# Block 0's first root among the second half's work, and two weight conversions behind the low parts, by a table of issue places

## The chip, the cores and the metric

The kernel runs on one core of a Trainium2 chip. The metric is the time of one execution on the device, in microseconds (us); lower is better. A core has a matrix engine (PE, TensorE), a vector engine (DVE), a scalar engine (ACT), a general engine (POOL, GpSimd) and SP, whose queue issues all the transfers (DMAs) of this kernel. Each engine takes its instructions in the order in which the program issues them; between engines there are only semaphores.

## The reference

Three stages follow each other: attention over 2 x 8 heads of 768 positions (a local window and one key per block of 32), a gated layer with a root-mean-square norm, and a second layer with an ELU.

```python
def _moe_ref(x, w_gate, w_val, w_out, rms_g):
    rms = np.sqrt(np.mean(x * x, axis=-1, keepdims=True) + 1e-06)
    xn = x / rms * rms_g
    g = xn @ w_gate
    silu = g * (1.0 / (1.0 + np.exp(-g)))
    return (silu * (xn @ w_val)) @ w_out          # 1536 tokens, 512 -> 1536 -> 512

def _moe2_ref(x, w_in, w_out):
    h = x @ w_in                                  # 512 -> 2048 -> 512
    return np.where(h > 0.0, h, np.exp(np.minimum(h, 0.0)) - 1.0) @ w_out
```

## The kernel before

**Blocks.** The 1536 tokens are three blocks of 512 columns, with the model dimension on the partitions. Block 0 goes through attention first. Its two halves of 256 tokens (`slice(0, 256)` and `slice(256, 512)`, called the first and the second half here) enter the gated layer as soon as each is there. Blocks 1 and 2 go through attention under the matmuls of block 0, and later through the two layers together.

**The gated layer on block 0.** Every float32 operand is cut into a high and a low part: `x_hi` (ACT or DVE) and `x_lo` (DVE) for the tokens, `split_a` (ACT) and `split_b` (POOL or DVE) for the weights. `project` multiplies high by high, high by low and low by high, 12 matmuls of 128 x 256 for one half of 256 tokens. The first products of chunks 0 and 1 run a half at a time, in PSUM banks of their own: `pv0_1c`, `pv0_0c`, `pg0_1`, and later `pg0_0`.

**The root.** The norm's factor for one half is computed in a row of small steps, `add_norm`: `square` (ACT), `sum_square` (PE, 16 float32 matmuls with 4 columns, bank `m0`), `mean_square` (DVE, frees the bank), `root` (POOL, a power), `diagonal` (DVE, two instructions), `spread` (PE, two float32 matmuls, bank `t0` for the first half and `t1` for the second), `keep_root` (DVE, copies the factor to `rk0` and frees the bank). On block 0 the factor is first used by `gate_r`, which needs both halves.

**The weights.** They come as 64-bit floats. `fetch` (SP) loads a piece into one of five buffers `st`; `convert_a` (ACT), `convert_b` and `convert_d` (DVE) make a 32-bit word of it in a buffer `raw`. `convert_b` writes the word from the upper half of the 64 bits; `convert_d` adds the lowest bits from the lower half, and is the last to read the `st` buffer. `keep` (SP) writes the word to memory for the later blocks, and `split_a`, `split_b` make the parts for the matmuls.

**What sets the order.** `Order.issue` (lines 82 to 217) plays the steps through on a timetable of costs and due times before anything is emitted, notes the order in which they start (`started`), and then calls them in that order. The order of these calls is the order of each engine's instructions. The semaphores are put in by the tile framework, from the order of the calls too: a step waits for every earlier call that wrote what it reads, or that read or wrote what it writes; a buffer passes on when all the steps of its last tile are done. The bank of each tile is the one that the timetable chose.

**The order around the change.** On PE: `turn_e` of pair 3, `sum_square` (first half), `scores` of pair 4 (banks `t0`, `t1`), `apply_v2` of pair 3, `pv0_1c` (first half), `spread` (first half, bank `t0`), `pv0_0c` and `pg0_1` (first half), `pv0_0c` and `pg0_1` (second half), `turn_e` of pair 4 twice, `sum_square` (second half), `pg0_0` (first half), `apply_v2` of pair 4 (bank `t0`), `spread` (second half), `pg0_0` (second half). On DVE: `convert_b` of v0, g1, g0, then `convert_d v 0`, `convert_d g 0`, the four `x_lo` of the first half with `mean_square` between, `convert_d g 1`, `diagonal`, `add_mask`, `row_max`, `keep_root`, `row_max`, the four `x_lo` of the second half. On ACT, `split_a` of g1 stands before the four `x_hi` of the second half. `keep v 0`, `split_a` and `split_b` of v0 are called right behind `convert_d v 0`, ahead of the last `x_lo`.

Of the kernel before, what the change touches and what calls it, by code (L numbers as in the profile page):

```python
# [43 lines left out]
class Order:  # L44
# [18 lines left out]
    def add(self, engine, cost, due, fn, *args, r=(), w=(), new=()):  # L63

        due += SHIFT.get((fn.__name__, sum(due >= x for x in EDGES)), 0)
        self.ops.append((engine, cost, due, fn, args, tuple(r), tuple(w), tuple(new)))
# [15 lines left out]
    def issue(self):  # L82
        ops = self.ops
        n = len(ops)
        before = [set() for _ in range(n)]
        writer, readers, home, maker, users = {}, {}, {}, {}, {}
        queue = {}
        for i, (engine, _, due, _, _, r, w, new) in enumerate(ops):
            for tag, name in new:
                home[name] = tag  # L90
                if tag in self.slots and self.slots[tag][1]:
                    queue.setdefault(tag, []).append((due, i, name))
            for key in r:
                before[i].add(writer[key])
                readers.setdefault(key, []).append(i)
            for key in w:
                if key in writer:
                    before[i].add(writer[key])
                before[i].update(readers.pop(key, ()))
                writer[key] = i  # L100
            before[i].discard(i)
            for name in {key.split("#")[0] for key in (*r, *w)} | {name for _, name in new}:
                if name in home:
                    before[i].add(maker.setdefault(name, i))
                    users.setdefault(name, set()).add(i)
            before[i].discard(i)
        queue = {tag: [name for _, _, name in sorted(x)] for tag, x in queue.items()}
        after = [[] for _ in range(n)]
        left = [len(b) for b in before]
        for i, b in enumerate(before):  # L110
            for j in b:
                after[j].append(i)

        ready_at = [op[2] if op[0] in ("SP", "-") else 0.0 for op in ops]
        free = {tag: bufs for tag, (bufs, _) in self.slots.items()}
        busy, soon, started, port = dict(self.busy), {}, [], 0.0
        dma_free = now = 0.0
        events = [(t, -1, 0) for t in (*ready_at, *busy.values()) if t > 0]
        heapq.heapify(events)
        taken = [None] * n  # L120
        ticks = {}
        tiled = 0

        def offer(i):
            for engine in ops[i][0] if isinstance(ops[i][0], dict) else (ops[i][0],):
                soon.setdefault(engine, []).append(i)

        for i in range(n):
            if not left[i]:
                offer(i)  # L130


        def pick(i):
            need, found = {}, []
            for tags, name in ops[i][7]:
                for tag in tags if isinstance(tags, tuple) else (tags,):
                    n = need.get(tag, 0) + 1
                    if free[tag] >= n and (not self.slots[tag][1] or name in queue[tag][:n]):
                        break
                else:  # L140
                    return None
                need[tag] = n
                found.append((tag, name))
            return found

        def can(i):
            return pick(i) is not None

        def shared(i, engine):
            return engine in ("DVE", "POOL") and ops[i][3].__name__ in SHARED  # L150

        while len(started) < n or events:
            for engine in list(soon):
                if busy.get(engine, 0.0) > now + 1e-9:
                    continue
                todo = sorted((i for i in soon[engine] if taken[i] is None), key=lambda i: (ops[i][2], i))
                best = next((
                    i for i in todo if ready_at[i] <= now + 1e-9 and can(i)
                    and (not shared(i, engine) or port <= now + 1e-9)), None)
                if best is None:  # L160
                    continue
                where, cost, due, _, _, _, _, new = ops[best]
                if isinstance(where, dict):
                    cost = where[engine]
                look = now + self.look * cost
                if engine != "SP" and any(
                        ops[i][2] < due - self.urgent and now < ready_at[i] <= look and can(i) for i in todo):
                    continue
                taken[best] = engine
                for e in where if isinstance(where, dict) else (where,):  # L170
                    soon[e].remove(best)
                for tag, name in pick(best):
                    home[name] = self.tag_of[name] = tag
                    free[tag] -= 1
                    if self.slots[tag][1]:
                        queue[tag].remove(name)
                if engine == "SP":
                    dma_free = max(now + self.DMA_START, dma_free) + cost
                    busy[engine] = now + self.ISSUE.get(ops[best][3].__name__, 0.42)
                    end = dma_free + self.DONE.get(ops[best][3].__name__, self.DMA_DONE)  # L180
                else:
                    if engine == "PE":
                        name = ops[best][3].__name__
                        start = now
                        if TILED.get(name, 0) != tiled:
                            tiled = TILED.get(name, 0)
                            start += DRAIN_IN if tiled else DRAIN_OUT
                        end = self.pe_end(start, cost, LIGHT.get(name, 1.0), ticks)
                    else:
                        end = now + cost  # L190
                    busy[engine] = end
                if shared(best, engine):
                    port = end
                heapq.heappush(events, (end + (0.2 if engine == "PE" else 0.13), best, 1))
                heapq.heappush(events, (busy[engine], -1, 0))
                started.append(best)
                for j in after[best]:
                    left[j] -= 1
                    ready_at[j] = max(ready_at[j], end + self.hop(engine, ops[j][0]))
                    if not left[j]:  # L200
                        offer(j)
                        heapq.heappush(events, (ready_at[j], -1, 0))
            if not events:
                stuck = [(e, [(ops[i][2], ops[i][3].__name__, ops[i][4][:3]) for i in t[:3]]) for e, t in soon.items()]
                raise RuntimeError(f"no group can start: {stuck} {free}")
            now, i, ends = heapq.heappop(events)
            if ends:
                for name in {key.split("#")[0] for key in (*ops[i][5], *ops[i][6])} | {x for _, x in ops[i][7]}:
                    if name in users:
                        users[name].discard(i)  # L210
                        if not users[name]:
                            del users[name]
                            free[home[name]] += 1
        for i in started:
            ops[i][3](*((taken[i],) if isinstance(ops[i][0], dict) else ()), *ops[i][4])
        return now


# [1 line left out]
def fused_kernel(ctx: ExitStack, tc: tile.TileContext, q, k, v, w_gate, w_val, w_out, rms_g, w_in2, w_out2, out):  # L220
# [720 lines left out]
    def add_act(src, dst, due, tag="act"):  # L941
        h, l = dst + "h", dst + "l"
        add(ANY_SB, 0, due, act_a, src, dst, tag, r=[src], w=[h], new=[(tag, h)])
        add(ANY_2[ACT_B if "act1_0" in dst else 0], 0, due + 0.6, act_b, src, dst, tag, r=[src, h], w=[l], new=[(tag, l)])

# [641 lines left out]
X_0 = 23.0, 30.0  # L1587
WARM_AT = (3.4, 3.9, 4.0, 7.5, 8.5, 9.5, 10.5, 13.0)
AFTER_K, WARM_LONG = {1: 0, 2: 2}, {1: 8}
ACT_B = 0  # L1590
LO_0, LO_1 = (1, 1, 0), 0
LEN_A, LEN_2, LEN_U, LEN_P = 9.3, 6.3, 9.7, 1.37
# [40 lines left out]
```

## Time and profile before

| | us |
|---|---|
| median of 3 runs | 590.31 |
| lowest and highest | 589.7, 591.51 |
| the profiled execution | 590.2 |
| its span, first to last instruction | 588.4 |

The profile is one execution. Times in it are counted from the first instruction. What lies around the span is 1.8 us. A row of the timeline gives start, duration, engine, line, operation, result and operands, how many instructions are merged in it, and in brackets the idle time before it with what ended it. Buffer numbers are left out of the names, so that `pv_0c` is `pv0_0c`, `pg` is any `pg0_n`, and a tile of the root shows as the slice in its name.

### The profile page before, as it was taken

What the parts mean: (1) busy time and instruction counts of PE and PEld (TensorE: products, weight loads), DVE (VectorE), ACT (ScalarE), POOL (GpSimd) and SP (SyncE); (2) the same over time, 40 slices, a digit from 0 to 9 for tenths busy, and PEclk for the clock granted to TensorE, in tenths of its full rate; (3) what the DMA queues carried; (4) which work ended last, traced back from release to release, by engine and by line L of the source; (5) the groups of instructions that cost most, each with busy time, mean ns of one, the idle gap of its engine ahead of it and who ended that gap; (6) DMA issues with size and microseconds to landing.
All of it is one profiled execution on the core that took longest, in us unless ns stands there. A gap on an engine that the chain in (4) does not pass through costs nothing.

```text
span 588.4 us, 10067 instructions
## 1 busy us (share of the span) xinstructions
PE 575.3 (98%) x3382; PEld 469.9 (80%) x3382; DVE 543.4 (92%) x1048; ACT 408.4 (69%) x888; POOL 97.1 (17%) x144
## 2 busy tenths in 40 slices
PE   7899999999999999999999999999999999999997
PEld 3688877888888888888888888788888888888886
DVE  4999988889999997999989888999999999999994
ACT  4887749755989888375455446596667599977651
POOL 5655466453311104000000000000000000000000
PEclk9999999999999999999999999999999999999999
DMA  9688997769778699223533453331206625816021
GB/s 318 227 282 299 321 381 279 252 204 298 251 260 299 230 378 342 99 101 116 178 107 108 144 164 123 90 108 55 72 19 206 187 73 173 261 58 207 1 72 53
DMA packets 56052, 108.80 MB, mean 185 GB/s; under 512 B 6784, under 2 KB 19584, under 8 KB 56000
## 3 DMA queue, kind: packets, MB, share of 16 engines
q1 hardware_dynamic: 56000, 108.16, 55.4%
q8 instruction: 26, 0.43, 0.3%
q14 instruction: 26, 0.21, 0.1%
HBM read 79.82 MB, written 28.31 MB: 184 GB/s over the span
## 4 chain that ended last, share of the span: by engine, by line
PE 87%; DVE 7%; ACT 3%; issue 1%; DMA 1%; POOL 0%; DVEq 0%; ACTq 0%; POOLq 0%
PE acc L952 13%; PE ph L896 8%; PE B_1u L1123 7%; PE B_2u L1123 6%; PE B_2d L1302 6%; PE A_1u L1123 5%; PE C_1u L1123 5%; PE B_1d L1302 4%; PE pg L896 4%; PE A_2u L1123 4%; PE C_2d L1302 4%; PE C_2u L1123 4%; PE A_2d L1302 4%; PE C_1d L1302 3%; ACT e L670 2%; PE A_1d L1302 2%
## 5 line engine op out<-in xcount | busy, mean ns | idle before, releaser
L1123 PE MATMUL B_1u<-xh,w_1u 128*128 128x512 f32 x144 | 48.9, 389 | 0.0
L896 PE MATMUL ph<-xa,ws_i 128*128 128x512 f32 x192 | 45.9, 392 | 0.0
L896 PEld LDWEIGHTS ph<-xa,ws_i 128*128 128x128 f32 x192 | 35.7, 188 | 7.7 <-issue 0.2
L896 PE MATMUL pg<-xs,ws_g 128*128 128x512 f32 (+1 forms) x168 | 36.9, 366 | 0.2 <-DVE th L920 0.2
L1123 PE MATMUL C_1u<-xh,w_1u 128*128 128x512 f32 x96 | 33.4, 390 | 1.1 <-DVE c_1u L1115 1.1
L303 ACT CAST wd<-rd 128x512 fp32r<-128x512 f32 x49 | 29.6, 618 | 5.5 <-PE A_1d L1302 2.8
L1123 PE MATMUL A_1u<-xh,w_1u 128*128 128x512 f32 x96 | 33.2, 389 | 0.0
L314 DVE TENSOR_TENSOR wd<-rd,wd 128x512 fp32r<-128x512 f32 x49 | 33.0, 684 | 0.0
L1302 PE MATMUL B_2d<-td,wd 128*128 128x512 f32 x144 | 32.8, 389 | 0.0
L1123 PE MATMUL B_2u<-xh,w_2u 128*128 128x512 f32 x96 | 32.8, 391 | 0.0
L896 PEld LDWEIGHTS pg<-xs,ws_g 128*128 128x128 f32 x168 | 27.9, 189 | 5.8 <-POOL ws_g L314 0.6
L1302 PEld LDWEIGHTS B_2d<-td,wd 128*128 128x128 f32 x144 | 27.0, 188 | 5.6
L1123 PEld LDWEIGHTS B_1u<-xh,w_1u 128*128 128x128 f32 x144 | 27.0, 188 | 5.6
L303 ACT CAST td<-z 128x512 fp32r<-128x512 f32 x28 | 16.7, 620 | 16.9 <-DVE z L1284 16.7
L1123 PE MATMUL B_1u<-xl,w_1u 128*128 128x512 f32 x72 | 28.0, 389 | 0.0
L685 POOL TENSOR_TENSOR e<-e,rs 128x480 f32<-128x480 f32 x20 | 21.3, 1070 | 38.8 <-ACT ex L930 16.7
L670 ACT ACTIVATE e<-e,nm 128x120 f32<-128x120 f32 x64 | 24.4, 385 | 0.9 <-DVE nm L663 0.9
L1302 PE MATMUL B_1d<-td,wd 128*128 128x512 f32 x108 | 24.6, 389 | 0.0
L1302 PEld LDWEIGHTS B_1d<-td,wd 128*128 128x128 f32 x108 | 20.3, 188 | 4.2
L303 ACT COPY h_1u<-B_1u 128x512 f32<-128x512 f32 x22 | 12.9, 588 | 14.8 <-PE B_1u L1123 13.5
L1302 PE MATMUL A_2d<-td,wd 128*128 128x512 f32 x96 | 22.2, 389 | 0.0
L1123 PEld LDWEIGHTS C_1u<-xh,w_1u 128*128 128x128 f32 x96 | 18.0, 188 | 5.3 <-DVE c_1u L1115 1.6
(530 smaller groups left out, 1770.2 us busy)
## 6 DMA issues: line engine op xcount, KB each, us to landing
st_i<-in_moe_w_in SPq DMA_DIRECT2D x16, 512.0 KB, 4.9
st_p<-in_moe_w_out SPq DMA_DIRECT2D x16, 512.0 KB, 5.4
st_v<-in_moe_w_val SPq DMA_DIRECT2D x12, 512.0 KB, 5.0
st_g<-in_moe_w_gate SPq DMA_DIRECT2D x12, 512.0 KB, 6.5
st_o<-in_moe_w_out SPq DMA_DIRECT2D x12, 512.0 KB, 5.2
kept_p<-raw_p SPq DMA_DIRECT2D x16, 256.0 KB, 5.1
kept_i<-raw_i SPq DMA_DIRECT2D x16, 256.0 KB, 5.2
va<-in_v SPq DMA_DIRECT2D x20, 192.0 KB, 6.4
```

Source lines behind the costliest of these rows:

```text
L303: nc.scalar.copy(out=out, in_=in_)
L314: (nc.gpsimd if eng == POOL else nc.vector).tensor_sub(out, a, b)
L670: nc.scalar.activation(out=e[:, pr, :], in_=s[:, pr, :], func=AF.Exp, bias=nm[:, pr:pr + 1], accum_out=ss[:, pr:pr + 1])
L685: nc.gpsimd.tensor_mul(e, e, rs.unsqueeze(2).to_broadcast([P, NP, NK]))
L896: nc.tensor.matmul(pt[:, i], wt[:, a, kk * P:(kk + 1) * P], xt[:, c, i], start=(kk == 0 and n == 0), stop=(kk == KM - 1 and n == 2))
L952: nc.tensor.matmul(acc, wt[:, a, cs], ot[e], start=(first and n == 0), stop=(last and n == 2))
L1123: nc.tensor.matmul(pt, wt[:, a, cs], xt[e][:, kk], start=first and kk == n == 0, stop=kk == 1 and n == 2, skip_group_check=not first)
L1302: nc.tensor.matmul(pt[:, h], wt[:, a, cs], xt[:, e, h], start=first and n == 0, stop=last and n == 2 and h.stop == TB, skip_group_check=i ...
```

## The change

`issue` now moves single calls behind others. A table `HOLD` has pairs: a step, and the step right behind which it is called. `find` takes the first started step of that name with those arguments; `emit` calls a step and then, at once, those held by it. Nothing else of the timetable is changed: banks and buffers are those that it chose, and the steps that are not named keep their places among each other.

```diff
+        def find(name, *some):
+            return next(i for i in started if ops[i][3].__name__ == name and set(some) <= set(map(str, ops[i][4])))
+
+        held = {}
+        for late, first in HOLD:
+            held.setdefault(find(*first), []).append(find(*late))
+        later = {j for x in held.values() for j in x}
+
+        def emit(i):
+            ops[i][3](*((taken[i],) if isinstance(ops[i][0], dict) else ()), *ops[i][4])
+            for j in held.get(i, ()):
+                emit(j)
+
         for i in started:
-            ops[i][3](*((taken[i],) if isinstance(ops[i][0], dict) else ()), *ops[i][4])
+            if i not in later:
+                emit(i)
...
+HOLD = [
+    (("sum_square", "0", "slice(0, 256, None)"), ("project", "pv0_0c", "slice(256, 512, None)")),
+    (("mean_square", "0", "slice(0, 256, None)"), ("copy_e", "0", "4_0")),
+    (("root", "0", "slice(0, 256, None)"), ("mean_square", "0", "slice(0, 256, None)")),
+    (("diagonal", "0", "slice(0, 256, None)"), ("convert_b", "g", "2")),
+    (("spread", "0", "slice(0, 256, None)"), ("project", "pg0_0", "slice(0, 256, None)")),
+    (("convert_d", "v", "0"), ("x_lo", "xT0", "3", "slice(0, 256, None)")),
+    (("convert_d", "g", "0"), ("x_lo", "xT0", "3", "slice(0, 256, None)")),
+    (("keep_root", "0", "slice(0, 256, None)"), ("convert_d", "o", "2")),
+]
```

In the new order PE has `sum_square` (first half) behind `pv0_0c` (second half), and `spread` (first half) between `pg0_0` (first half) and `apply_v2` of pair 4. DVE has `mean_square` between the two `copy_e` of pair 4, `diagonal` behind `convert_b g 2`, `keep_root` between `convert_d o 2` and `convert_d g 2`, and `convert_d v 0`, `convert_d g 0`, `convert_d g 1` in a row behind the last `x_lo` of the first half. `keep v 0`, `split_a` and `split_b` of v0 are now called before `convert_d v 0`, so they take the words as `convert_b` left them, without the lowest bits of this one piece of the value weights.

## Rows read from the trace of the kernel before

**Rows 1.** Busy time by stretch: sum of the stretches from 53 us on.

```profile
sum 535.40, PE 530.10 PEld 434.59 DVE 501.07 ACT 370.68 POOL 65.45; mean PE 88.35 PEld 72.43 DVE 83.51 ACT 61.78 POOL 10.91
```

**Rows 2.** Timeline of PE, 32 to 51 us (start, us, engine, line, operation).

```profile
32.85 0.51 PE L785 MATMUL 0slice(0, 256, None)_702<-ones,)slice(0, 256, None)_656 128*128 128x4 f32 x4
...
34.62 0.64 PE L654 MATMUL s<-ka,q 64*64 64x120 f32 x15
...
38.76 0.70 PE L820 MATMUL 0slice(0, 256, None)_808<-0slice(0, 256, None)_794,ones 128*128 128x256 f32 x2 [0.38 <-DVE e L659]
...
40.73 1.60 PE L896 MATMUL pg<-xs,ws_g 128*128 128x256 f32 x12
42.17 1.60 PE L896 MATMUL pv_0c<-xs,ws_v 128*128 128x256 f32 x12
...
45.05 1.34 PE L695 MATMUL at<-ident,e 128*120 128x128 f32 x8
46.23 0.51 PE L785 MATMUL lice(256, 512, None)_928<-ones,lice(256, 512, None)_834 128*128 128x4 f32 x4
...
47.93 1.68 PE L896 MATMUL pg<-xs,ws_g 128*128 128x256 f32 x12
49.54 0.68 PE L707 MATMUL pv<-ats,va 120*64 120x64 f32 x15
...
50.62 0.70 PE L820 MATMUL lice(256, 512, None)_995<-lice(256, 512, None)_990,ones 128*128 128x256 f32 x2
```

**Rows 3.** Timeline of ACT: `copy_e` of pair 3 and `split_a` of g1.

```profile
33.98 0.57 ACT L303 COPY ats<-at 120x512 f32<-120x512 f32 x1
...
37.82 0.62 ACT L303 CAST ws_g<-raw_g 128x512 fp32r<-128x512 f32 x1 [0.42 <-DVE raw_g L455]
```

**Rows 4.** Timeline of POOL: `split_b` of v0 and of g1.

```profile
35.15 1.28 POOL L314 TENSOR_TENSOR ws_v<-raw_v,ws_v 128x512 fp32r<-128x512 f32 x1 [3.37 <-ACT ws_v L303]
...
38.70 1.29 POOL L314 TENSOR_TENSOR ws_g<-raw_g,ws_g 128x512 fp32r<-128x512 f32 x1
```

**Rows 5.** SP: its wait before `keep v 0`, that issue, and times to landing.

```profile
SPq L469 <- DVE raw_v L455: 0.9, 1, 0.9
...
33.77 0.35 SPq L469 DMA_DIRECT2D kept_v<-raw_v  x1
...
DMA to landing us min/median/max: 3.9/3.9/3.9
...
L606 SPq DMA_DIRECT2D va<-in_v x2: 313/314/315, 32.0 to 32.5; - x2
...
DMA to landing us min/median/max: 4.6/4.6/4.6
```

**Rows 6.** Timeline of DVE, 37 to 50 us: the kinds of steps that move.

```profile
37.03 0.75 DVE L455 SCALAR_TENSOR_TENSOR raw_g<-st_g,raw_g 128x512 uint16<-128x512 uint16 x1
...
39.76 0.41 DVE L305 COPY rk<-0slice(0, 256, None)_808 128x256 f32<-128x256 f32 x1
...
40.65 1.66 DVE L876 SCALAR_TENSOR_TENSOR xs<-xT,g_sb,xs 128x256 fp32r<-128x256 f32 x4
...
45.68 1.44 DVE L305 COPY ats<-at 120x512 f32<-120x512 f32 x2 [1.13 <-PE at L695]
...
48.31 0.15 DVE L790 TENSOR_SCALAR lice(256, 512, None)_960<-lice(256, 512, None)_928 128x2 f32<-128x2 f32 x1
...
49.01 0.74 DVE L455 SCALAR_TENSOR_TENSOR raw_g<-st_g,raw_g 128x512 uint16<-128x512 uint16 x1
49.63 0.42 DVE L442 TENSOR_SCALAR raw_v<-st_v 128x512 uint32<-128x512 uint32 x1
49.96 0.48 DVE L806 TENSOR_SCALAR lice(256, 512, None)_990<-ident,lice(256, 512, None)_963 128x128 f32<-128x128 f32 x2
```

**Rows 7.** Timeline of PE at the start: idle matmuls (`keep_warm`), 128x512, bf16.

```profile
4.73 3.57 PE L1413 MATMUL warm<-idle_w 128*128 128x512 bf16 x8
...
11.56 1.46 PE L1413 MATMUL warm<-idle_w 128*128 128x512 bf16 x6
```

## The prediction

> **What bounds the kernel now.** I read the page first: PE is busy almost throughout, the other engines less. Then the busy time by stretch: behind 53 us PE is idle for 535.40 - 530.10 = 5.3 us in all [rows 1], so what PE loses before that is hardly won back. The changed steps lie between 31 and 53 us, so I read that stretch engine by engine in the timeline, and the waits beside it. On PE the reader is to see a gapless row: from `sum_square` of the first half at 32.85 to `spread` of the second at 50.62 one idle time is shown, 0.38 us ahead of the first `spread` (38.76), and `turn_e` with `sum_square` behind it takes 1.18 us (45.05 to 46.23) where 8 transposes need some 1.0 [rows 2]. More than about 0.6 us there is not to be won; the question is what each moved step drags along.
>
> **The changes, part by part.** The order of calls decides both an engine's order and what a step waits for, so I go down PE's new order and ask what is ready.
>
> (1) *`sum_square` leaves 32.85.* Behind it stood `scores` at 34.62 [rows 2]. These write banks `t0` and `t1`; `t1` is held by the transposes of pair 3 until ACT's `copy_e` has read them, and that ran from 33.98 to 34.55 [rows 3]. It hangs on nothing that moves. So the 16 small matmuls lay in a hole that stays: `scores` still start at 34.6, and PE is idle there for some 1.6 us. Gain: nothing. (At worst for this step the hole alters the clock: a rival below. A gain is excluded as long as `copy_e` stays where it is.)
>
> (2) *`spread` leaves 38.76.* PE finished `pv0_1c` 0.38 us earlier [rows 2], at 38.38, and now takes `pv0_0c` at once. Twelve matmuls are 1.44 us apart from the next group (40.73 to 42.17 [rows 2]), so PE is free at 39.82 instead of 40.73: 0.91 us early.
>
> (3) *The two `convert_d`.* Ahead of the four `x_lo` they cost DVE two times 0.63 us (49.01 to 49.63 [rows 6]); without them the `x_lo` end before 36, but PE cannot begin `pv0_1c` earlier than before, by (1), so this wins nothing. Behind them, `convert_d v 0` overwrites words that `split_a`, `split_b` and `keep` of v0 now read first. It must wait for all three, and in DVE's queue stand behind it `convert_d g 0`, `convert_d g 1`, the masks and maxima of pair 4 and the second half's `x_lo`. `split_b` ends at 35.15 + 1.28 = 36.43 [rows 4]. `keep` waited 0.9 us for the conversion and was issued at 33.77 [rows 5]; without that wait it is issued at 32.87. When it lands is the unknown. It landed 3.9 us after its issue [rows 5], at 37.67. The same 3.9 us would give 36.8; the transfer of `va` before it, issued at 32.5, landed 4.6 us later, at 37.1 [rows 5], and landings follow the order of issue here. Bounds: 36.5 (`split_b` decides) and 37.7 (it lands as before). I take 37.4, a little behind `va`, nearest to the rows of its neighbours.
>
> By the Trainium skill ("DMA: Bandwidth & Descriptors", the anatomy of one DMA) a transfer takes some 2.0 us and its bytes at 436 GB/s, an estimate of 2.6 us for these 256 KB. By that rule the landing would be at 35.5, `split_b` would decide, and the sum below would be 3.5 us instead of 4.4. The trace has 3.9 us for this transfer, and I go by that.
>
> From 37.4: 0.63 + 0.63 + 0.75 [rows 6] puts the end of `convert_d g 1` at 39.41; before, it was 37.03 + 0.75 = 37.78 [rows 6]. ACT's `split_a` of g1 began at 37.82 and takes 0.62 [rows 3], POOL's `split_b` 1.29 [rows 4]: 39.45 + 0.62 + 0.08 + 1.29 = 41.44, and `pg0_1` starts at 41.5, not at 40.73 [rows 2]. So **+0.77 us**, with PE idle for 1.7. By the bounds -0.1 to +1.1. `x_hi` of the second half stands behind `split_a` on ACT and moves by 1.63 as well; its `x_lo` (1.66 for four [rows 6]) then end near 43.4, in time for the last products of `pv0_0c`, which starts at 42.9. Nothing is added there.
>
> SP too: `fetch o 2` and `fetch g 2` need the `st` buffers that the two conversions free, and go out some 2.5 us later. Their `convert_a` on ACT comes well behind and itself moves by 1.6. I cost that at nothing; if ACT did wait there, `split_a` of g2 behind it has to wait for `convert_d g 2` anyway.
>
> (4) *`sum_square` comes back* behind `pv0_0c` of the second half, where PE has no hole. The second half's one took 46.23 to 47.93, 1.70, and the matmuls behind it 1.61 (47.93 to 49.54) instead of 1.44 [rows 2]. **+1.87 us**. PE reaches `turn_e` of pair 4 at 45.05 + 0.77 + 1.87 = 47.69. What the transposes wait for, exponentials and POOL's scaling, has moved by 1.63 only.
>
> (5) *Bank `m0`.* The second half's `sum_square` may start only when `mean_square` has read the first's, and that now stands behind `copy_e`. `copy_e` began 0.63 us after `turn_e` (45.05, 45.68) and takes 0.72, `mean_square` 0.15 [rows 2, 6], 1.46 with semaphores, where 1.18 lay between `turn_e` and `sum_square` [rows 2]. **+0.28 us**. `root` and `diagonal` run beside `sum_square` and `pg0_0`; POOL has the place.
>
> (6) *Bank `t0`.* Between `pg0_0` and `apply_v2` stands `spread` (0.70 to its end [rows 2]), and `apply_v2` needs the bank that `keep_root` frees (0.41 [rows 6]). With semaphores **+1.19 us**. DVE has by then done `convert_d o 2` and waits, so nothing shortens it.
>
> (7) *`diagonal` of the second half* comes on DVE behind `keep_root`, `convert_d g 2` (0.63), `convert_b v 2` (0.33) and takes 0.48 [rows 6], 1.36 after `keep_root`; `apply_v2` covers 1.08 (49.54 to 50.62 [rows 2]). **+0.27 us**.
>
> Sum: 0.77 + 1.87 + 0.28 + 1.19 + 0.27 = **4.4 us**, with `spread` of the second half at 55.0 instead of 50.62. By the bounds of (3) 3.5 to 4.7. The profiled execution took 590.2, so 594.6 for it; it stands 0.1 under the median of the runs, so 594.7 there.
>
> **Rivals.** *(A) No wait for `keep`* (the words written later do not hold DVE). Then (3) leaves PE its 0.91 us and the sum is -0.91 + 1.87 + 0.28 + 1.19 + 0.27 = 2.7: 593.0. For it: nothing in the trace of before shows such a wait. Against: the buffer is read by three steps called earlier.
>
> *(B) The hole costs the clock.* PE idles for 1.6 us behind a stretch of small matmuls. At the start, 8 idle matmuls took 3.57 us and later 6 took 1.46 [rows 7], 0.446 and 0.243 each: the two levels, 1.2 and 2.4 GHz. Such a slow stretch again would add 8 x 0.203 = 1.6 us: 596.3. Against: the page shows the granted clock full throughout, over the gaps that PE has before 31 us too. The Trainium skill ("TensorE: Matmul & The Clock Gate", "What's actually happening") has it that the throttled state is the default and activity releases it; no row of before shows a fall by which to test that here.
>
> *(C) Not slower: the delay is taken up later.* If PE's 5.3 us of idle time behind 53 us [rows 1] are waits for things that do not move, a late PE finds them done, and up to all of the 4.4 us is given back: about 590. It decides from 2.6 us given back. For it: the transfers run close to their limit in the stretch behind 53 us. Against: those waits name DVE and ACT, with results of PE's own matmuls, which move along, and the rest is the tail.
>
> **How the numbers follow.** Forecast 0.66 (593.4 to 595.2), A 0.13, B 0.06, C 0.10, and 0.05 for a gain that I do not see. 0.3%, about what a measurement of this kernel can tell from no change, is 1.8 us. Slower by more: forecast, A and B, 0.85. Within: most of C, 0.11. Faster: 0.04. The range, 592.4 to 596.0, has the forecast and A, leaving out B, C and the unseen gain, 0.2 in all.
>
> **What would show it.** In the profile after: PE idle for about 1.6 us ahead of `scores` at 34.6, released by ACT's `copy_e` (1); DVE idle from about 35 to 37.4 ahead of `convert_d v 0`, released by a DMA (3), and PE idle ahead of `pg0_1`; `sum_square` of the second half waiting for DVE (5), `apply_v2` waiting for `keep_root` (6), and `spread` of the second half at 55.0. Wrong if `scores` start before 34, if `convert_d v 0` starts before 36, or if the late PE gains on the old timetable behind 60 us.

## The result, and the profile after

The changed kernel takes 596.65 us (median of 4 runs, 595.59 to 598.93) where the kernel before, beside it, takes 590.74 (589.7 to 591.51): 1.0102 times as long, interval 1.0081 to 1.0124. It is slower, as forecast, by 5.9 us and not 4.4, and 0.65 us above the end of the range. The profiled execution took 596.64, its span is 594.90, and the clock was granted in full throughout.

The timeline of PE after, 33 to 57 us (start, us, engine, line, operation, result and operands, in brackets the idle time before and what ended it; line numbers behind `issue` are higher by 14), answers to [rows 2]:

```profile
33.74 0.65 PE L709 MATMUL at<-ident,e 128*120 128x128 f32 x4
35.51 1.52 PE L668 MATMUL s<-ka,q 64*64 64x120 f32 x32 [1.11 <-ACT xT L317]
36.97 1.15 PE L721 MATMUL pv<-ats,va 120*64 120x64 f32 x32
...
41.83 0.50 PE L910 MATMUL pg<-xs,ws_g 128*128 128x256 f32 x2 [0.65 <-ACT ws_g L317]
43.19 1.46 PE L910 MATMUL pg<-xs,ws_g 128*128 128x256 f32 x10 [0.86 <-POOL ws_g L328]
44.49 1.60 PE L910 MATMUL pv_0c<-xs,ws_v 128*128 128x256 f32 x12
45.93 0.50 PE L799 MATMUL 0slice(0, 256, None)_863<-ones,)slice(0, 256, None)_656 128*128 128x4 f32 x4
...
49.15 1.03 PE L709 MATMUL at<-ident,e 128*120 128x128 f32 x8
50.69 0.58 PE L799 MATMUL lice(256, 512, None)_922<-ones,lice(256, 512, None)_815 128*128 128x4 f32 x4 [0.50 <-DVE 0slice(0, 256, None)_916 L804]
...
55.09 1.15 PE L721 MATMUL pv<-ats,va 120*64 120x64 f32 x32 [0.52 <-DVE rk L319]
56.76 0.67 PE L834 MATMUL lice(256, 512, None)_995<-lice(256, 512, None)_990,ones 128*128 128x256 f32 x2 [0.52 <-DVE lice(256, 512, None)_990 L820]
```

Where before one idle time of 0.38 us was shown [rows 2], there are now six, and each is at a place that the prediction names: ahead of `scores`, of `pg0_1` (two), of the second `sum_square` (waiting for `mean_square`), of `apply_v2` (for `keep_root`) and of the second `spread` (for `diagonal`). Ahead of `scores` the row names another releaser than the prediction: 1.11 us until ACT has copied `xT` and so freed `t0`. Only two of the 32 matmuls run then; the others, from 35.99 on, wait for `copy_e` of pair 3 as predicted (it ends at 35.94).

DVE in the same trace, four of its steps (against [rows 6]), then POOL at 55 to 58 us, then SP's `keep v 0` with its time to landing (against [rows 5]):

```profile
38.81 0.76 DVE L469 SCALAR_TENSOR_TENSOR raw_v<-st_v,raw_v 128x512 uint16<-128x512 uint16 x1 [2.75 <-POOL va L616]
...
55.91 0.70 DVE L820 TENSOR_SCALAR lice(256, 512, None)_990<-ident,lice(256, 512, None)_963 128x128 f32<-128x128 f32 x2
56.53 1.76 DVE L328 TENSOR_TENSOR ws_o<-raw_o,ws_o 128x512 fp32r<-128x512 f32 x1
...
58.56 0.41 DVE L319 COPY rk<-lice(256, 512, None)_995 128x256 f32<-128x256 f32 x1
```
```profile
55.85 0.61 POOL L614 MEMSET va<- 32x512 f32 x1 [1.79 <-PE pv L721]
56.44 1.32 POOL L328 TENSOR_TENSOR ws_g<-raw_g,ws_g 128x512 fp32r<-128x512 f32 x1
```
```profile
L483 SPq DMA_DIRECT2D kept_v<-raw_v x1: 378/378/378, 34.3 to 34.3; - x1
...
DMA to landing us min/median/max: 4.4/4.4/4.4
```

`convert_d v 0` starts at 38.81 after 2.75 us of idle DVE; `keep v 0`, issued at 34.26, landed at 38.71. The profile puts the wait down to POOL's memset, which ended at 38.76. In the ten other traces of kernels with this move (and with `keep` ahead of it) the start lies 0.10 us behind the landing of `keep`, while the memset ends before it or after it, and the profile names the transfer itself; here the row of the execution that took 597.31:

```profile
38.62 0.75 DVE L469 SCALAR_TENSOR_TENSOR raw_v<-st_v,raw_v 128x512 uint16<-128x512 uint16 x1 [2.86 <-DMA kept_v<-raw_v]
```

So it is the transfer that DVE waits for. The other two marks, `diagonal` at 0.70 us and `split_b o 0` at 1.76 us, come back below.

Before a single moved step there is a difference already: `turn_e` of pair 3 starts at 33.74, and at 32.36 before, where PE has

```profile
32.36 0.65 PE L695 MATMUL at<-ident,e 128*120 128x128 f32 x4
...
35.60 1.15 PE L707 MATMUL pv<-ats,va 120*64 120x64 f32 x32
```

(the second of these rows is `apply_v2` of pair 3). So the stretch is counted from there: from `turn_e` of pair 3 to `spread` of the second half 18.27 us before, 23.02 after, 4.75 more. What is left of the 6.45 us between the spans is 1.38 ahead of it and 0.32 behind it. Busy time by stretch behind it, from 59.5 us on, the sum as in [rows 1]:

```profile
sum 535.40, PE 530.00 PEld 434.26 DVE 502.06 ACT 371.37 POOL 65.47; mean PE 265.00 PEld 217.13 DVE 251.03 ACT 185.68 POOL 32.74
```

PE is idle for 5.4 us there, and for 5.3 before: nothing is given back. Three questions follow: are the terms in the stretch the forecast's, does the late start belong to the change, and what do the other runs lose, since this execution is not among the long ones.

### The profile page after: what moved, and what is told of

Read it like the earlier page. It is cut to its first block, busy times and chain, and to the rows that moved or that the text cites. A ratio compares the mean times of both kernels' runs of the same rounds, so it can differ in the third digit from the quotient of the medians.

```text
span 594.9 us, 10071 instructions
## 1 busy us (share of the span) xinstructions
PE 576.2 (97%) x3382; PEld 469.5 (79%) x3382; DVE 544.0 (91%) x1048; ACT 408.4 (69%) x888; POOL 97.7 (16%) x144
## 4 chain that ended last, share of the span: by engine, by line
PE 85%; DVE 6%; DMA 4%; ACT 3%; issue 1%; SPq 0%; POOL 0%; DVEq 0%; ACTq 0%; POOLq 0%
PE acc L966 13%; PE ph L910 7%; PE B_1u L1137 7%; PE B_2u L1137 6%; PE B_2d L1316 5%; PE A_1u L1137 5%; PE C_1u L1137 5%; PE B_1d L1316 4%; PE pg L910 4%; PE C_2d L1316 4%; PE A_2u L1137 4%; PE C_2u L1137 4%; PE A_2d L1316 4%; PE C_1d L1316 3%; PE A_1d L1316 2%; DMA vtok<-in_v 2%
```

## Experiments: the terms in the stretch

**The two kernels once more.** Neither kernel is changed.

> The kernel before, profiled once more. In the trace of the changed kernel everything is already 1.4 us late at 31 us, ahead of the first moved step. Theory 1: that is how this execution's first loads fell, and has nothing to do with the change; then this trace, too, may reach turn_e of pair 3 anywhere from 32.3 to 33.8 us, and the stretch from the start of that turn_e to the start of the second half's spread on PE is 18.3 us again (32.36 to 50.62 in the first trace of before). Theory 2: the start is late in every execution of the changed kernel; then this trace has turn_e within 0.3 us of 32.36.

> The changed kernel, profiled once more. By theory 1 turn_e of pair 3 starts anywhere from 32.3 to 33.8 us (33.74 in its first trace); by theory 2 at 33.7. By both the stretch from that turn_e to the second half's spread is 23.0 us, 4.8 longer than before.

Before: 591.22, the stretch 18.26, and `turn_e` at 31.75. After: 597.68, the stretch 22.25, `turn_e` at 34.71. In these two pairs of traces the stretch repeats to 0.01 us in the old order and varies by 0.8 in the new one; the start varies in both. Of the 0.8, 0.5 lie in the hole ahead of `scores`: in the second trace of the changed kernel the clock was at half from 30.7 to 34.1 us, PE came late to `turn_e`, and the hole behind it was shorter (`turn_e` to `apply_v2` 2.68 us and not 3.22).

**The six steps of the root alone**, and **the two conversions alone.** The table loses the lines of the other part:

```diff
-    (("convert_d", "v", "0"), ("x_lo", "xT0", "3", "slice(0, 256, None)")),
-    (("convert_d", "g", "0"), ("x_lo", "xT0", "3", "slice(0, 256, None)")),
```

> Only the six steps of the first half's root are moved; the two convert_d stay where they were. My sum without its term (3): PE gets pv0_0c 0.9 us early and loses 1.8 for sum_square, 0.4 at bank m0, 1.1 at bank t0 and 0.6 at diagonal (the sizes of the trace of after): 2.9 to 3.0 us over before in the stretch, so 21.2 us from turn_e to spread, and a time 3 us over before. The rival that the whole loss sits in the conversions' wait would give before's time within 1 us.

> Only convert_d v 0 and convert_d g 0 are moved behind the last x_lo; the root stays where it was. By my term (3) convert_d v 0 waits until about 37.4 for keep's transfer (times on before's axis), diagonal and the mask that frees bank t0 come behind, and the first half's spread starts at 40.4 instead of 38.8: 1.7 us over before in the stretch (20.0 us). The rival that the conversions cost nothing by themselves, since DVE is only reordered, gives 18.3 us and before's time.

The first of them is the change without the part shown; in the second the table has these two lines alone, and as in the change `split_a` and `split_b` of v0 then work without the lowest bits. The root alone: 596.36, ratio 1.0077 (1.0047 to 1.0107). The conversions alone: 594.41, ratio 1.0061 (1.0035 to 1.0086). Both times are above what was expected, but each of these two profiled executions has a time at half the clock within the stretch. From `apply_v2` of pair 3 to the second `spread` they take 19.63 and 18.32 us, and the kernel before 15.02; less 1.6 us for such a time (below: 1.4 to 1.8) the growth is some 3.0 and 1.7 us, near what was expected. In the root alone the half clock lies from 49.8 to 53.2 us, and the other steps show their sizes without it: PE is at the second half's `pv0_0c` 0.75 us earlier than before, loses 1.78 for `sum_square`, 0.36 at bank `m0` and 0.58 at `diagonal`. In the second one DVE, then PE:

```profile
37.37 0.76 DVE L469 SCALAR_TENSOR_TENSOR raw_v<-st_v,raw_v 128x512 uint16<-128x512 uint16 x1
```
```profile
40.59 0.92 PE L834 MATMUL 0slice(0, 256, None)_808<-0slice(0, 256, None)_794,ones 128*128 128x256 f32 x2 [1.99 <-DVE e L673]
```

`convert_d v 0` at 37.37, `keep` landed at 37.27; and the `spread` that was left in its old place waits 1.99 us for the mask that is queued behind the conversions on DVE.

**`keep v 0` behind the conversion**, so that DVE no longer waits for a transfer:

```diff
+    (("keep", "v", "0"), ("convert_d", "v", "0")),
```

> The change, and keep v 0 is held behind convert_d v 0 as well, so that the conversion no longer waits for that transfer, only for split_a and split_b of v0. The stretch is read on PE from apply_v2 of pair 3 to the second half's spread: 15.0 us in both traces of before, 19.8 and 19.6 in the two of after. If the transfer is what term (3) waits for, convert_d v 0 starts 0.9 us earlier, right behind split_b, and the stretch is 18.9 us. If the wait is split_b's, or the framework's, it stays at 19.7.

```profile
36.89 0.75 DVE L469 SCALAR_TENSOR_TENSOR raw_v<-st_v,raw_v 128x512 uint16<-128x512 uint16 x1 [1.80 <-POOL ws_v L328]
```

Now `split_b` of v0 is named, and it is the one. From `apply_v2` of pair 3 to the second half's `pv0_0c` PE takes 6.50 us, where the change took 6.79 to 7.62 in its five traces without a fall of the clock in the stretch (7.52 and 7.30 in the first two), and the kernel before 6.57: between 0.3 and 1.1 us won, where 0.9 was expected. The whole stretch, 19.45, can't be held against the 18.9 that was expected, since the clock was at half from 51.6 to 55.0 us in it. Time 595.77, ratio 1.0088 (1.006 to 1.0116), whose interval overlaps the change's.

**The first half's root in a bank of its own** (both PSUM tiles in `m1`, not `m0` and `t0`):

```diff
-        tag = o.tag_of.get(name, tag)
+        tag = MINE.get(name) or o.tag_of.get(name, tag)
```

> The change, with the first half's sum_square and spread written to bank m1, which is free then, in place of m0 and t0. The 0.5 us that the second sum_square waits for mean_square fall away. The 0.5 us that apply_v2 waits for keep_root fall away too, but by my step (7) spread of the second half then waits longer for diagonal, which stands on DVE behind keep_root, so that only 0.2 of it is won: a stretch of 19.1 us. If both waits are really won, 18.7; if the banks have nothing to do with them, 19.7.

```profile
50.46 0.51 PE L799 MATMUL lice(256, 512, None)_922<-ones,lice(256, 512, None)_815 128*128 128x4 f32 x4
...
54.20 1.15 PE L721 MATMUL pv<-ats,va 120*64 120x64 f32 x32
56.29 0.67 PE L834 MATMUL lice(256, 512, None)_995<-lice(256, 512, None)_990,ones 128*128 128x256 f32 x2 [0.94 <-DVE lice(256, 512, None)_990 L820]
```

Both bank waits are gone, (5) for good; that of (6) is mostly taken over by the wait for `diagonal`, 0.94 us, so that from `sum_square` to `spread` only 0.24 us is won (5.83 against 6.07). The whole stretch is 20.56 where 19.1 was expected; the clock was at half from 42.9 to 46.3 us in it. Time 597.72, ratio 1.01 (1.0063 to 1.0136).

**Only `diagonal`, `spread` and `keep_root` moved**, with `sum_square` in its old place. This asks whether the hole ahead of `scores` stays when `sum_square` leaves.

> Only diagonal, spread and keep_root of the first half are moved to the places of the change; sum_square, mean_square, root and the two conversions stay where they were. Against the run with the whole root moved, this puts the 16 matmuls back into the hole ahead of scores. By my steps (1), (4) and (5) that is worth 1.8 + 0.4 us, which leaves 0.8 us over before: a stretch of 15.8 us. If there is no hole and PE's work merely changes places, the stretch stays at 18.0, 3 us over before. A fall of the clock in the stretch adds up to 1.7 in either case.

The stretch from `apply_v2` of pair 3 to the second `spread` is 16.34, near the 15.8 of the theory that the hole stays and far from 18.0. The half microsecond over the 15.8 is in this row:

```profile
46.99 0.65 PE L709 MATMUL at<-ident,e 128*120 128x128 f32 x4 [0.72 <-POOL e L699]
```

PE comes to `turn_e` of pair 4 early and waits there for POOL's scaling of the exponentials. Time 593.64, ratio 1.0049 (1.0028 to 1.007).

**The kernel before with one bank changed**, so that its only shown wait, 0.38 us ahead of the first `spread`, goes:

```diff
+MINE = {"prs0slice(0, 256, None)": "m1"}
```

> The kernel before with one thing other: the row that spread of the first half writes takes bank m1 in place of t0. Nothing is moved. My theory: the 0.38 us that PE waited ahead of that spread is gone and nothing is late in its place, so the stretch from apply_v2 of pair 3 to spread of the second half is 14.6 to 14.7 us and not 15.0, and the time about 0.4 us lower, 590.2 beside 590.6. The rival: pv0_0c, which follows, waits for the same 0.38 us, and nothing changes.

```profile
38.98 0.69 PE L820 MATMUL 0slice(0, 256, None)_808<-0slice(0, 256, None)_794,ones 128*128 128x256 f32 x2
...
46.48 0.65 PE L695 MATMUL at<-ident,e 128*120 128x128 f32 x4 [0.64 <-POOL e L685]
```

The wait is gone, and the same wait for the exponentials is there instead. The stretch, 16.49, holds a time at half the clock, from 49.3 us on, and is no measure. Ratio 1.001 (0.9997 to 1.0023): nothing won, and neither theory had this row. In this order what PE wins ahead of `turn_e` of pair 4, that step takes back.

## Experiments: what lies outside the sum

**Idle matmuls in the holes.** Seventeen matmuls whose results nothing reads, 5, 6, 2, 2 and 2 of them behind `turn_e` of pair 3, the first half's `pv0_0c`, `turn_e` of pair 4, the first `spread` and `apply_v2`:

```diff
+            nc.tensor.matmul(pt, idle_w, idle_w.unsqueeze(1).to_broadcast([P, 4, P]), start=True, stop=True)
```

> The change, with 17 idle matmuls (128x512, bf16, into bank m1, their result unused) in the five holes that the trace of after shows on PE: 5 behind turn_e of pair 3, 6 behind pv0_0c (first half), 2 each behind turn_e of pair 4, behind the first spread and behind apply_v2 of pair 4. They take 0.22 us each, less than the holes. If the time over my sum comes from a clock that falls, at random, where PE idles, no fall is seen behind 30 us, the stretch stays at 19.7 to 19.9 and the runs gather at the low end of those of after, 595.6 or below, with a median about 1 us under it. If the clock has no part, the median stays at 596.7 or rises.

597.24, ratio 1.0096 (1.0068 to 1.0124), not lower. Busy time by stretch (start and end, us, busy time of each engine with its number of instructions, then PEclk, the granted clock):

```profile
29.00:32.80 3.80, 3.68 (x50) 3.17 (x52) 2.92 (x9) 3.32 (x12) 1.97 (x2) 0.55 0.34 85
32.80:53.00 20.20, 19.48 (x214) 17.06 (x209) 14.78 (x36) 14.28 (x39) 9.38 (x11) 1.00 0.82 272
53.00:56.70 3.70, 3.70 (x35) 2.50 (x35) 2.01 (x6) 0.62 (x1) 0.55 (x2) 0.54 0.69 232
```

At two places the clock was granted at 1.2 and not at 2.4 GHz, each time for some 3.4 us ((1 - 0.54) / 0.5 x 3.7), the second one while PE was busy without a gap. The first lies ahead of the first filled hole; the second does not, so filling the holes did not keep the clock from falling.

**More runs and more traces of both kernels.**

> The changed kernel again, to see what is left of its 5.9 us when the stretch itself accounts for 4.75. Theory of the fall of the clock: a run without a fall has a span 4.8 to 5.3 us above an unfallen run of before, and falls (about 0.7 to 1.7 us each) occur in more of its runs than of before's. Theory of the start: with the clock full throughout, the spans stand 5.5 us and more above before's, and turn_e of pair 3 starts behind 33 us again (32.36 before). Theory of chance: the median of more runs comes down to some 595.5, with as many falls as before has.

> The kernel before once more, for its start. If the start of turn_e of pair 3 varies from execution to execution, it stands anywhere from 31.5 to 34 us here; if the changed order is what makes it late, it is at or under 32.4 as in the two traces of before so far. The stretch from apply_v2 of pair 3 to spread of the second half is 15.0 either way without a fall of the clock.

> The changed kernel once more, for its start, beside the look at the kernel before. If the changed order makes the start late, turn_e of pair 3 starts behind 33 us as in its two traces so far (33.74 and 34.71); if the start varies by execution, it may as well be at 32. The stretch from apply_v2 of pair 3 to spread of the second half is 19.6 to 19.8 without a fall of the clock, and about 1.6 more with one in it.

> The kernel before, for its start and its clock. Start by execution, whatever the kernel: turn_e of pair 3 anywhere from 31.5 to 34.5 us. Start made late by the changed order: under 33.6 us, as in the four traces so far that have the old order (31.75 to 33.51). A fall of the clock, if there is one, at 29 to 56 us in both cases, and about 1.6 us on the stretch that it falls in.

> The changed kernel, for its start and its clock. Start by execution: turn_e of pair 3 anywhere from 31.5 to 34.5 us. Start made late by the changed order: 33.4 to 34.7 us, as in the four traces of it so far. Falls of the clock: one or two are likelier than none; the stretch from apply_v2 of pair 3 to spread of the second half 19.4 to 19.8 us, and about 1.6 more for each fall in it.

> As for the second look at the kernel before: start by execution 31.5 to 34.5 us, start made by the order under 33.6 us.

> As for the second look at the changed kernel: start by execution 31.5 to 34.5 us, start made by the order 33.4 to 34.7 us; stretch 19.4 to 19.8 us and about 1.6 for each fall of the clock in it.

The five more runs of the changed kernel have a median of 599.08, ratio 1.0128 (1.0109 to 1.0147): not the 595.5 of the theory of chance. Two of the five show no fall of the clock, and their spans, 598.1 and 596.1, stand 8.3 and 6.3 us above the median of the runs of before beside them that show none, beyond what the theory of the fall allowed (4.8 to 5.3). The single executions took 601.84, 597.31 and 595.37; those of the kernel before 591.4, 593.31 and 590.46. The longest, by stretch:

```profile
26.00:29.00 3.00, 1.58 (x10) 1.02 (x10) 2.90 (x9) 1.68 (x10) 2.32 (x5) 1.00 0.40 131
29.00:33.00 4.00, 3.82 (x57) 3.29 (x58) 3.12 (x8) 3.42 (x13) 1.97 (x2) 0.57 0.39 102
33.00:42.90 9.90, 7.35 (x111) 6.18 (x108) 6.87 (x15) 5.99 (x14) 3.89 (x6) 1.00 0.82 255
42.90:46.50 3.60, 3.60 (x19) 3.60 (x19) 2.98 (x9) 3.60 (x18) 0.82 (x1) 0.53 0.69 259
46.50:53.00 6.50, 6.00 (x53) 5.78 (x53) 2.97 (x9) 4.38 (x8) 3.67 (x4) 1.00 0.76 300
53.00:56.80 3.80, 3.80 (x20) 3.70 (x19) 1.61 (x4) 0.00 (x0) 1.03 (x1) 0.55 0.28 81
```

Three falls, two of them in the moved steps; from `turn_e` of pair 3 to the second `spread` it takes 25.90 us where the traces without a fall in it took 22.25 to 23.11, so a fall there costs 1.4 to 1.8 us. Of the 17 runs of the changed kernel 10 have a mean granted clock that shows a fall (0.997 or less; one fall is 1.7 of 595 us), six of them two or more (0.995 or less). Of the 62 runs of the kernel before beside the experiments 13 do, none two. Of 57 runs of the eight other altered kernels 35 do, in each kernel at least 4 in 9.

The traces show where. In the five of the kernel before the clock fell twice, from 28.6 and from 31.2 us, ahead of the moved steps. In the fifteen of altered kernels (the changed one among them) there are ten falls that begin between 40 and 54 us, in nine traces: seven at the end of the second half's `sum_square` or in the `pg0_0` behind it, three in the first matmuls behind a wait of 0.9 to 2.0 us. In the changed kernel's first trace PE did the same there at the full clock, so this says where it falls and not why.

The start: in five traces of the kernel before `turn_e` of pair 3 starts between 31.75 and 35.28 us, in seven of the changed one between 32.56 and 34.71. The ranges overlap, a trace of the changed kernel (32.56, the execution that took 595.37) is below what the theory of the order allowed, and each engine does the same steps in the same order up to this place in both kernels. So the start most likely belongs to the execution. That the difference of the means, 0.6 us, is nothing but scatter is not shown; the latest start of either kernel (35.28 and 34.71) has a fall of the clock right ahead of it.

**The collision on DVE and POOL.** Against the stretch, some traces lost another microsecond at one place: PE ahead of `pg0_3`. POOL's `split_b`, DVE's `guard` (the row `ss`) and PE in the execution of the changed kernel that took 597.31, then in the one of the kernel before that took 593.31, then POOL and DVE in the trace that [rows 1] are from:

```profile
64.65 1.66 POOL L328 TENSOR_TENSOR ws_g<-raw_g,ws_g 128x512 fp32r<-128x512 f32 x1 [2.46 <-ACT ws_g L317]
...
65.09 1.25 DVE L690 TENSOR_SCALAR ss<-ss 128x4 f32<-128x4 f32 x1
...
67.58 1.67 PE L910 MATMUL pg<-xs,ws_g 128*128 128x512 f32 x6 [0.60 <-DVE th L934]
```
```profile
60.95 1.68 POOL L314 TENSOR_TENSOR ws_g<-raw_g,ws_g 128x512 fp32r<-128x512 f32 x1 [2.58 <-ACT ws_g L303]
...
61.37 1.29 DVE L676 TENSOR_SCALAR ss<-ss 128x4 f32<-128x4 f32 x1
...
63.90 1.66 PE L896 MATMUL pg<-xs,ws_g 128*128 128x512 f32 x6
```
```profile
57.81 1.76 POOL L314 TENSOR_TENSOR ws_g<-raw_g,ws_g 128x512 fp32r<-128x512 f32 x1 [2.60 <-ACT ws_g L303]
...
58.23 0.16 DVE L676 TENSOR_SCALAR ss<-ss 128x4 f32<-128x4 f32 x1
```

`guard` is a step of 0.16 us on 4 columns; beside POOL's `split_b` it takes 0.16 in some executions and 1.25 to 1.29 in others. `split_b o 0` on DVE takes 0.69 us in the old order, where it begins ahead of the same kind of step of POOL (DVE, then POOL, in the trace of [rows 6]):

```profile
50.35 0.69 DVE L314 TENSOR_TENSOR ws_o<-raw_o,ws_o 128x512 fp32r<-128x512 f32 x1
```
```profile
50.87 1.67 POOL L314 TENSOR_TENSOR ws_g<-raw_g,ws_g 128x512 fp32r<-128x512 f32 x1
```

It takes 1.76 in six of seven traces of the new order, where it begins 0.09 us behind it (56.53 and 56.44, above). DVE is late by 1.1 us from either. From the second `spread` to `pg0_3` PE takes

| | `guard` 0.14 to 0.18 us | `guard` 1.25 to 1.29 us |
|---|---|---|
| `split_b o 0` 0.7 us | 10.04 (four of before, one of after) | 10.14 (one of before) |
| `split_b o 0` 1.76 us | 10.26 (two of after) | 11.02 to 11.09 (four of after) |

One late step is covered by PE's own work; with both, PE is 1.0 us late, and its wait names DVE (0.60 to 0.68 us). The other kernels' traces go the same way: with `guard` late alone 10.00 to 10.13 (three traces), with two late steps of DVE 11.05 to 11.07 (three; in one of them the first late step is the `convert_b` behind `split_b o 0`). The Trainium skill ("SBUF — State Buffer", "Who interferes with whom") states that DVE and GpSimd share a pair of memory ports, that a DVE step with two inputs in that memory contends with a GpSimd step that reads there, that one in a mode that takes both ports contends with GpSimd too, and that there the one that issues first has the pair for its whole length. The 1.76 us agree. For `guard` the last part does not show in these records: POOL's step begins 0.40 to 0.46 us ahead of it in every trace, and `guard` is late in some and not in others.

**The collision taken away.** Four more calls moved on DVE, and the changed kernel beside it:

```diff
+    (("diagonal", "0", "slice(256, 512, None)"), ("convert_d", "g", "2")),
+    (("split_b", "ws0_o0", "slice(0, 512, None)"), ("diagonal", "0", "slice(256, 512, None)")),
+    (("convert_b", "v", "2"), ("gate_r", "th0_1")),
+    (("convert_b", "g", "3"), ("gate_r", "th0_1")),
```

> The changed kernel with four more calls moved on DVE alone: the second half's diagonal right behind convert_d g 2, split_b o 0 right behind that, and convert_b v 2 and g 3 behind the first gate_r. So diagonal and split_b o 0 begin ahead of POOL's split_b g 2 and not beside it. My theory of what is left over (two collisions of DVE and POOL, 1.1 us each: split_b o 0 took 1.76 us and not 0.68 in all six traces of the changed kernel, guard of pair 5 1.25 to 1.29 us and not 0.16 in four of them; DVE can absorb one and not both): split_b o 0 takes 0.68 us, the second half's keep_root starts about 1.3 us earlier against the end of split_b g 2's old place, PE waits at most 0.1 us for gate_b ahead of pg0_3 even where guard is late, and from spread of the second half to the end it is 537.9 to 538.3 us, not 539.0; diagonal costs 0.3 us less on the path. Time 0.8 to 1.3 us under the changed kernel's. The rival, that what is lost behind the stretch has another cause: 538.8 to 539.0 us from spread to the end whatever split_b o 0 does, and at most 0.3 us won.

> The changed kernel beside it on the same chip, as the measure for the other one: split_b o 0 takes 1.76 us; where guard of pair 5 takes 1.25 us or more, PE waits about 0.6 us ahead of pg0_3 and from spread of the second half to the end it is 538.8 to 539.0 us; where guard takes 0.2 us, no such wait and 538.1 us unless something behind 70 us is late.

```profile
55.57 0.87 DVE L820 TENSOR_SCALAR lice(256, 512, None)_966<-ident,lice(256, 512, None)_963 128x128 f32<-128x128 f32 x2
55.95 0.70 DVE L328 TENSOR_TENSOR ws_o<-raw_o,ws_o 128x512 fp32r<-128x512 f32 x1
57.29 0.42 DVE L319 COPY rk<-lice(256, 512, None)_993 128x256 f32<-128x256 f32 x1 [0.64 <-PE lice(256, 512, None)_993 L834]
```

`split_b o 0` takes 0.70 us, and `keep_root` starts 0.71 us behind `spread` and not 1.80. `diagonal` still runs beside POOL's memset, and most of its price stays (PE waits 0.35 us for it, not 0.52). From `spread` to the end it is 537.97 us. But `guard` was on time in this execution, and in the one beside it (538.28), where behind a fall of the clock `split_b o 0` began ahead of POOL's step and took 0.69 us: neither trace holds the case that would have told the two theories apart. The times, 597.01 (595.07 to 598.64), ratio 1.0092 (1.0068 to 1.0115), and 597.8 (597.19 to 601.37), ratio 1.0125 (1.0091 to 1.0159), differ in the expected direction, with intervals that overlap. The price of the collision rests on the table above. No kernel here was faster than the one before.

## Why the prediction was right and wrong

Step by step, with the trace of [rows 2] against that of the result:

| step | forecast | measured | from |
|---|---|---|---|
| (1) hole ahead of `scores` stays | 0 | -0.01 | `turn_e` to `apply_v2` of pair 3: 3.24, 3.23 |
| (2), (3) `spread` out, DVE waits for `keep` | +0.77 | +0.95 | `apply_v2` to second `pv0_0c`: 6.57, 7.52 |
| (4) `sum_square` back | +1.87 | +1.78 | second `pv0_0c` to `turn_e`: 2.88, 4.66 |
| (5) bank `m0` | +0.28 | +0.36 | `turn_e` to `sum_square`: 1.18, 1.54 |
| (6) bank `t0` | +1.19 | +1.09 | `sum_square` to `apply_v2`: 3.31, 4.40 |
| (7) `diagonal` | +0.27 | +0.59 | `apply_v2` to `spread`: 1.08, 1.67 |
| sum | 4.4 | 4.75 | |

**Right:** each wait, its place and its releaser (ahead of `scores` in part), and that rival A does not hold: DVE waits for `keep`. In the five traces of the changed kernel without a fall in this stretch it grew by 3.98 to 4.84 us, mean 4.4. That the mean meets the forecast is partly luck: the term with the widest bounds, (3), was +0.2 to +1.05 in them, within its bounds of -0.1 to +1.1, and two other terms were off by 0.1 and 0.3. `keep` landed 3.7 to 4.6 us behind its issue in the traces with this move, and the trace's 3.9 was the right end to go by. The estimate of 2.6 us from the Trainium skill ("DMA: Bandwidth & Descriptors") was too low each time; the 2.0 us and 436 GB/s stand there as a fit for transfers issued by GpSimd, and this one is issued by SP. Rival C did not come: nothing was given back behind 60 us.

**Mis-sized:** (7). `diagonal` was costed at its 0.48 us of [rows 6]. It took 0.70, beside POOL's `zero_v` (the memset at 55.85, begun 0.06 us ahead of it; before, the memset begins 0.34 us behind it), which makes 0.22 of the 0.32 us that were missed; the rest are the semaphores ahead of `spread`, which were not counted. Two of the prediction's sums do not come out as written, 1.36 in (7) and 1.46 in (5), where the parts named make 1.44 and 1.50: DVE's steps overlap by some 0.08 us, which it took off without saying so.

**Failed:** the sum ended at `spread` of the second half, as if a late PE could only stay as late as it is: what the delay sets off behind it stood at nothing, without a reason, and the falls of the clock were left out of the sum as a rival of 0.06. Over all traces of both kernels, in us (each column counts from the one before it):

| mean of | `turn_e`, pair 3, starts | to `spread` | to `pg0_3` | to the end | span |
|---|---|---|---|---|---|
| 5 traces before | 33.09 | 18.31 | 10.06 | 528.13 | 589.59 |
| 7 traces after | 33.67 | 23.28 | 10.68 | 528.63 | 596.25 |
| difference | 0.6 | 5.0 | 0.6 | 0.5 | 6.7 |

All runs give much the same: a median of 597.85 in 17 runs against 591.21 in 62, 6.6 us. Of the 6.7:

- 4.4 are the sum.
- 0.6 are falls of the clock in two of the seven stretches. Rival B's price, 1.6 us, was about right for one fall, but not its place (none of them begins in the hole ahead of `scores`), and 0.06 was the chance of a thing that always or never happens, where falls show in more than half of the runs and should have been a term with a mean price.
- 0.6 are the two collisions with POOL behind `spread`, a step that the prediction does not have, though `split_b o 0` stands in DVE's order right behind the moved `diagonal`.
- 0.6 are the start, which the traces do not tell from scatter.
- 0.5 lie behind `pg0_3`, in two of the seven traces (+3.1 and +2.0) as in one of five before (+1.6). In the one with +3.1 PE waits for a load at 86 us (`vtok`, 0.59 us shown), behind it for DVE and POOL; in the one of before for DVE and POOL, near 215 and 232 us. Why only in a few executions of either kernel is left open.

The falls are not the whole miss: the runs without one have medians of 596.66 (7 of the changed kernel) and 591.03 (49 of before), 5.6 us apart, and three of the four runs of the result are among them. In the profiled execution of the result the 2.0 us over the 594.6 forecast for it are the start (1.38), the terms (0.35) and what lies behind `spread` (0.32).

Open is what brings the clock down. Each altered kernel has falls in a larger share of its runs than the kernel before; the kernel before with one bank changed had them in 6 of 12 runs, with no call moved and a wait of 0.64 us put into the same stretch. So holes in it look like the cause, but this is not shown, and the filled holes did not mend it.

**Step (2)** came out, but only because `sum_square` comes back behind it. In the root alone PE kept its 0.75 us, since `turn_e` of pair 4 came 1.78 us later by (4). With `sum_square` in its old place `turn_e` took back 0.7 of the 1.06 us won, and in the kernel before with one bank changed all of it. The prediction gives no such condition.

## What to carry to other kernels

Count a moved step's waits beyond the last moved step, through what its engine meets behind it: a delay shifts the engines against each other, and steps of DVE and POOL that ran one after the other meet. A step that is to overwrite a buffer waits for the outgoing transfer that reads it, and its engine's whole queue with it. Where an engine has a hole that one wait sets, moving work out of the hole wins nothing, and moving it into a gapless stretch costs its full length. Time that an engine wins early is kept only if the next step's inputs are there by then.

## What the runs showed of the hardware that was not expected

- The granted clock fell to half for some 3.4 us at a time in kernels whose first traces show it full throughout: the mean clock shows a fall in 13 of 62 runs of one and 10 of 17 of the other, and two falls in the moved steps cost 2.8 to 3.6 us. In the traces a fall lies between 28 and 57 us, behind a stretch with PE at half busy (1.58 of 3 us) as well as in the middle of twelve matmuls in a row (53.1 us in the trace with the filled holes).
- A DVE step of 0.16 us on 4 columns takes 1.25 to 1.29 us beside POOL's subtraction of two 128x512 tiles, in 5 of 12 traces of the two kernels. POOL's step takes 1.66 to 1.78 us and not 1.29 in either case.
- `diagonal`'s two DVE instructions took 0.70 and 0.87 us where POOL's memset began just ahead of or between them, and 0.48 where it began 0.34 us behind the first.
